# Attention numerators as products of 64 weight columns for each half of the partitions

## The chip, the cores and the metric

The kernel runs on one core of one Trainium2 chip. The metric is the device time of one execution in microseconds (us). Three runs of the kernel before took 924.83, 926.39 and 926.86 us; the median, 926.39 us, is the time before.

## The reference, cut to what matters

Three parts follow one another: a linear attention with random features, a feed-forward block with silu, and a gated feed-forward block. The change is in the attention. Its shapes are batch 4, 8 heads, 576 tokens, head dimension 64 and 128 features.

```python
q_p, k_p = (phi(q_s), phi(k_s))              # exp of a projection, less its row maximum
kv = np.einsum('bhsm,bhsd->bhmd', k_p, v)    # sums over the tokens of k and v
z = np.sum(k_p, axis=2)
num = np.einsum('bhsm,bhmd->bhsd', q_p, kv)  # the numerators
den = np.einsum('bhsm,bhm->bhs', q_p, z)[..., None] + 1e-06
return (num / den).astype(np.float32)
```

After it, `x = moe(x)` and `out = moe2(x)` are large matrix products (2304 tokens, width 512, inner widths 2048 and 1536).

## The kernel before, in words

**Tiling of the attention.** Two heads lie side by side on the 128 partitions (a pair), and two batches are taken together: a unit `u` is one pair of heads with two batches of 576 tokens, so 1152 tokens, which are nine chunks of 128. There are eight units, so 72 chunks, and the loop `step(s)` (L913) takes one chunk a step. As 576 is four and a half chunks, the fifth chunk of each unit holds the last 64 tokens of one batch and the first 64 of the next. The helper `runs` (L692) cuts a stretch of tokens at that border and gives, for each batch, its range `a` to `z` within the chunk.

**A step.** `proj(s + 1)` (L749) projects q and k of the next chunk: six products into a bank of PSUM, taken in turn out of five (`bank`, L669). `soft(s)` (L760) takes the four row maxima on DVE (L765) and four exponentials on ACT (L769), which read that bank. `kv_tr(s - 2)` (L779) adds the chunk's k to the sums of k and v (L789; 128 feature columns as weights, 65 columns of v with a column of ones as moving data) and turns q by two transposes (L805); ACT copies the turned q to SBUF (L816). On GpSimd (POOL), `split_piece` (L701) splits the loaded q and k into a high and a low part (L706, L708). Each engine works in the order in which the program gives it work. Between steps `feed` (L508) adds operations of the next stage: conversion of weights (POOL sums at L376, DVE operations at L350, L357, L406 and L419) and of the attention's output (POOL at L601, ACT at L571, DVE at L580). How many of them a step takes depends on the step's number, not on a clock.

**The numerators.** When the sums of a batch are complete, DVE copies them to SBUF (`kv_evac`, L821) as a 128 by 130 tile `st`: for each of the two heads 65 columns, of which one is the sum z. Then `tail` (L896) plans three groups of three chunks for each unit: `num(u, g)` (L835) makes the products, `divide` (L852) adds a small number to the sums, inverts and multiplies on DVE, two steps later `turn` (L864) transposes the result, and `take_out` (L870) copies it to SBUF. In `num`, the turned q of a chunk is the weight operand (128 features by up to 128 tokens) and `st` of that batch and head is the moving operand of 65 columns. The result stands at the tokens' partitions `a` to `z` of a PSUM bank, with 130 columns for each chunk. A chunk within one batch takes two products with 128 weight columns, one for each head. The fifth chunk takes four products with 64 weight columns: the two heads of the first batch on partitions 0 to 63, then the two heads of the second batch on partitions 64 to 127. The operands are fp32, and the hardware makes two weight loads and two products of each source product, so the trace has 320 records at L843 for 160 source products.

**The end of the attention.** For the last unit, `last_nums` (L994) makes two groups in one go when the next stage has begun, and two more products (`mark`, L1043) follow that wait for `divide`. The following stages are matrix products at L1066 and L1433, emitted in an order that a planner with fixed costs lays down before the run.

Of the kernel before, what the change touches and what calls it, by code (L numbers as in the profile page):

```python
# [42 lines left out]
def kernel(  # L43
# [13 lines left out]
    nc = tc.nc  # L57
    ctx.enter_context(tc.manual_schedule())
    P = 128
    DM, NT = outT.shape  # L60
    D, M = omT.shape
# [12 lines left out]
    VH = D + 1  # L74
# [607 lines left out]
    raw, hl, kq, qp, kvps = {}, {}, {}, {}, {}  # L682
# [9 lines left out]
    def runs(lo, hi):  # L692
        for b in range(lo // S, (hi - 1) // S + 1):
            a, z = max(lo, b * S), min(hi, (b + 1) * S)
            yield b, a - lo, z - lo, a == b * S, z == (b + 1) * S
# [123 lines left out]
    st = {}  # L819
# [15 lines left out]
    def num(u, g, to=None):  # L835

        pxs[u, g] = x = px.popleft() if to is None else to
        acc = ps[x]
        for c in range(g * GC, (g + 1) * GC):
            for b, a, z, _, _ in runs(c * P, (c + 1) * P):  # L840
                for h in range(2):
                    o = (c - g * GC) * VW + h * VH
                    nc.tensor.matmul(  # L843
                        acc[a:z, o : o + VH],
                        qp[u][:, h, c * P + a : c * P + z],
                        st[u, b][:, h * VH : (h + 1) * VH],
                        start=True,
                        stop=True,
                        skip_group_check=True,
                    )  # L850

    def divide(u, g):  # L852
        acc = ps[pxs[u, g]][:, : GC * VW].rearrange("p (c w) -> p c w", w=VW)
# [42 lines left out]
    def tail(u, b, s):  # L896
        if b and u == NU - 1:
            return
        for g, a in ((1, s + 2), (2, s + 6)) if b else ((0, s + 2 - (u == NU - 1)),):
            at(a, num, u, g)  # L900
            at(a, lambda g=g: dve_q.append(lambda: divide(u, g)))
            at(a + 2, turn, u, g)
            at(a + 2, lambda g=g: dve_q.append(lambda: take_out(u, g)))
            if g == GC - 1:
                at(a + 4, store, u)
# [88 lines left out]
    def last_nums():  # L994

        u = NU - 1
        num(u, 1, 7)
        num(u, 2, 6)
        divide(u, 1)
        divide(u, 2)  # L1000
        nc.scalar.activation(silu, silu, AF.Silu)
        clk["PE"] += 1.8
        clk["ACT"] = max(clk["ACT"], clk["PE"]) + 1.5
        clk["DVE"] = max(clk["DVE"], clk["PE"]) + 2.0
        actx.close()
        operands("rb")
        streams["x"].extend(to_come.pop(0)())
        later_on.append((5, lambda: last_turn(1)))
        later_on.append((7, lambda: last_turn(2)))
# [632 lines left out]
```

## Time and profile before

| what | value |
|---|---|
| median of three runs | 926.39 us |
| lowest and highest | 924.83 and 926.86 us |
| the profiled execution's own time | 926.11 us |
| its span, first to last instruction | 924.3 us |
| mean granted TensorE clock | 0.998 |
| DVE, ACT, POOL busy | 71%, 60%, 21% of the span |
| attention | from the start to about 150 us |

The engines are PE (TensorE's products), PEld (its weight loads, which overlap the products), DVE (VectorE), ACT (ScalarE), POOL (GpSimd) and SP (SyncE, which issues most DMAs). Ends of products are modelled, so for TensorE the starts are the safer reading: the distance from one start to the next is the time that the work took from the engine. A line such as L843 is a line of the kernel. A time in brackets behind a row is idle time of the engine ahead of that instruction, with what ended it.

### The profile page before, as it was taken

The page shows a single profiled execution, that of the slowest core. Times are in us where ns is not written, and L with a number is a line of the kernel's source. Part 1 is how long each engine was busy: PE and PEld are TensorE (multiplying, and loading weights), DVE is VectorE, ACT ScalarE, POOL GpSimd, SP SyncE. Part 2 cuts the span into 40 slices and gives each one's busy share as a digit, 9 for nine tenths or more (in the row PEclk, how much of TensorE's full clock was granted, in tenths as well). Part 3 has the DMA queues.
Part 4 walks back from the last instruction along what each step waited for, and adds up shares of the span by engine and source line. Part 5 has one row for each costly group of instructions (what it writes and reads, how often), then busy time and mean ns, then how long its engine had stood idle before and what let it go on. Part 6 is the DMA issues. An engine that isn't in the chain of part 4 may idle for free.

```text
span 924.3 us, 15768 instructions
## 1 busy us (share of the span) xinstructions
PE 905.0 (98%) x5591; PEld 895.3 (97%) x5591; DVE 657.7 (71%) x1055; ACT 558.4 (60%) x1190; POOL 197.0 (21%) x244
## 2 busy tenths in 40 slices
PE   8999999999999998999999999999999999999998
PEld 8999999999999998999999899999999999899998
DVE  4898986857574398586689899574747447968584
ACT  5788785876667675455457765554455447445453
POOL 6676951104343100000000014221303010000000
PEclk9999999999999999999999999999999999999999
DMA  7576515848989991715613755562626159371701
GB/s 218 183 235 208 174 50 197 271 157 275 317 291 358 349 382 58 232 55 163 206 43 109 244 164 187 174 201 79 213 68 222 47 184 314 114 240 52 237 16 69
DMA packets 109888, 169.94 MB, mean 184 GB/s; under 512 B 9200, under 2 KB 93808, under 8 KB 109808
## 3 DMA queue, kind: packets, MB, share of 16 engines
q1 hardware_dynamic: 108640, 168.33, 55.8%
q8 instruction: 44, 0.72, 0.3%
q10 hardware_dynamic: 1168, 0.59, 0.2%
q14 instruction: 36, 0.29, 0.1%
HBM read 107.02 MB, written 61.87 MB: 183 GB/s over the span
## 4 chain that ended last, share of the span: by engine, by line
PE 90%; DVE 4%; DMA 3%; ACT 2%; issue 1%; SPq 0%; DVEq 0%; ACTq 0%
PE ps L1066 43%; PE ps L1433 31%; PE ps L843 3%; PE ps L789 3%; PE ps L755 2%; PE ps L756 2%; PE ps L757 2%; PE ps L805 2%; DMA g_d<-fa 1%; PE ps L868 1%; DVE ra L1296 1%; DMA fa<-in_moe_w_in 1%; DVE ra L419 0%; DMA ra<-wu_val 0%; DVE fa L1124 0%
## 5 line engine op out<-in xcount | busy, mean ns | idle before, releaser
L376 POOL TENSOR_TENSOR fa<-fa 128x256 f32<-128x256 f32 x136 | 112.6, 841 | 529.0 <-DVE fa L357 301.3
L1066 PE MATMUL ps<-ra 128*128 128x384 f32 x840 | 156.3, 335 | 3.0 <-ACT ps L1083 3.0
L1066 PE MATMUL ps<-rb,ra 128*128 128x384 f32 x840 | 157.3, 340 | 0.0
L1066 PE MATMUL ps<-rc,ra 128*128 128x384 f32 x840 | 156.8, 339 | 0.0
L1066 PEld LDWEIGHTS ps<-ra 128*128 128x128 f32 x840 | 146.7, 188 | 4.3 <-ACT ps L1083 4.3
L1066 PEld LDWEIGHTS ps<-rb,ra 128*128 128x128 f32 x840 | 148.7, 188 | 0.3 <-ACT ps L1083 0.3
L1066 PEld LDWEIGHTS ps<-rc,ra 128*128 128x128 f32 x840 | 148.6, 188 | 0.1
L1083 ACT ACTIVATE ps<-ps 128x384 f32<-128x384 f32 x180 | 85.5, 476 | 88.7 <-PE ps L1066 82.1
L1140 DVE TENSOR_TENSOR fa<-fa,ps 128x384 f32<-128x384 f32 x120 | 66.2, 552 | 100.5 <-ACT ps L1083 78.1
L1292 ACT ACTIVATE ra<-fa 128x768 fp32r<-128x768 f32 x105 | 88.0, 844 | 81.2 <-PE ps L1433 64.4
L1296 DVE TENSOR_TENSOR ra<-fa,ra 128x768 fp32r<-128x768 f32 x105 | 100.5, 957 | 50.5 <-PE ps L1433 31.9
L1433 PE MATMUL ps<-ra,rb 128*128 128x384 f32 x720 | 129.4, 340 | 0.0
L1433 PEld LDWEIGHTS ps<-ra,rb 128*128 128x128 f32 x720 | 127.8, 189 | 0.8 <-DVE ra L1296 0.6
L1433 PE MATMUL ps<-ra 128*128 128x384 f32 x612 | 109.7, 337 | 6.7 <-DVE ra L1296 6.5
L1433 PEld LDWEIGHTS ps<-ra 128*128 128x128 f32 x612 | 106.7, 189 | 8.8 <-DVE ra L1296 8.0
L769 ACT ACTIVATE kq<-ps,nb 128x128 f32<-128x128 f32 x288 | 83.1, 403 | 25.3 <-DVE nb L765 24.1
L1433 PE MATMUL ps<-ra,rc 128*128 128x384 f32 x432 | 78.2, 340 | 1.6 <-DVE ra L1296 1.6
L1433 PEld LDWEIGHTS ps<-ra,rc 128*128 128x128 f32 x432 | 76.1, 188 | 2.7 <-DVE ra L1296 2.7
L1107 ACT ACTIVATE fa<-fa 128x384 f32<-128x384 f32 x84 | 43.8, 522 | 28.8 <-DVE fa L1140 28.5
L1316 DVE TENSOR_TENSOR fa<-ra,fa 128x768 f32<-128x768 f32 x63 | 60.1, 954 | 0.7
L1292 ACT ACTIVATE ra<-ra 128x768 fp32r<-128x768 f32 x42 | 35.5, 845 | 36.0 <-PE ps L1433 32.1
L1296 DVE TENSOR_TENSOR ra<-ra 128x768 fp32r<-128x768 f32 x42 | 40.2, 958 | 20.9 <-PE ps L1433 9.3
(100 smaller groups left out, 1227.6 us busy)
## 6 DMA issues: line engine op xcount, KB each, us to landing
g_d<-fa SPq DMA_DIRECT2D x168, 192.0 KB, 3.4
fa<-g_d SPq DMA_DIRECT2D x42, 384.0 KB, 4.4
ra<-g_d SPq DMA_DIRECT2D x42, 384.0 KB, 4.1
fa<-in_moe_w_out SPq DMA_DIRECT2D x28, 512.0 KB, 5.3
fa<-in_moe_w_in SPq DMA_DIRECT2D x16, 512.0 KB, 5.0
wd_out<-fa SPq DMA_DIRECT2D x14, 512.0 KB, 3.3
fa<-in_moe_w_gate SPq DMA_DIRECT2D x12, 512.0 KB, 3.9
fa<-in_moe_w_val SPq DMA_DIRECT2D x12, 512.0 KB, 5.2
```

The costliest lines, as they stand in the source:

```text
L376: f(blk(f"S{n}"), blk(l), blk(r))
L769: nc.scalar.activation(e[:, i, h * M : (h + 1) * M], ps[:, i, h * M : (h + 1) * M], AF.Exp, bias=nb[:, 2 * i + h : 2 * i + h + 1],)
L789: nc.tensor.matmul(acc[:, o : o + VH], e[a:z, 0, h * M : (h + 1) * M], v_t[u % 2][a:z, c, o : o + VH], start=first and h == 0, stop=last, ...
L843: nc.tensor.matmul(acc[a:z, o : o + VH], qp[u][:, h, c * P + a : c * P + z], st[u, b][:, h * VH : (h + 1) * VH], start=True, stop=True, sk ...
L1066: nc.tensor.matmul(ps[b][:, :N], cut(l, j * P, P), cut(r, j * N, N), start=start and c == 0, stop=stop and c == 5, skip_group_check=True,)
L1083: nc.scalar.activation(out() if callable(out) else out, src, AF.Copy)
L1107: nc.scalar.activation(b["t"], src, AF.Silu)
L1140: nc.vector.tensor_add(t, t if in_place else p5[n], ps[bank_][:, :N])
L1292: nc.scalar.activation(ops[s, p, k][0], src(), AF.Copy)
L1296: nc.vector.tensor_sub(l, src(), h.bitcast(F32))
L1316: (nc.gpsimd if eng == "POOL" else nc.vector).tensor_sub(z(PLACE[to]), z(PLACE.get(l, l)), z(PLACE.get(r, r)))
L1433: nc.tensor.matmul(ps[BANKS[p] + e][:, :N], cut(a, e * P, P), b, start=p in FIRST and i == 0 and c == 0, stop=p in LAST and i == fp - 1 an ...
```

## The change

In `num`, each product over the partitions `a` to `z` becomes one product for each 64 of them. A chunk within one batch now takes four source products with 64 weight columns: for the first head the partitions 0 to 63 and then 64 to 127, then the same for the second head. The fifth chunk of a unit is cut as before. The sums of k and v (L789) keep 128 weight columns.

```diff
                 for h in range(2):
                     o = (c - g * GC) * VW + h * VH
-                    nc.tensor.matmul(
-                        acc[a:z, o : o + VH],
-                        qp[u][:, h, c * P + a : c * P + z],
-                        st[u, b][:, h * VH : (h + 1) * VH],
-                        start=True,
-                        stop=True,
-                        skip_group_check=True,
-                    )
+                    for i in range(a, z, D):
+                        nc.tensor.matmul(
+                            acc[i : i + D, o : o + VH],
+                            qp[u][:, h, c * P + i : c * P + i + D],
+                            st[u, b][:, h * VH : (h + 1) * VH],
+                            start=True,
+                            stop=True,
+                            skip_group_check=True,
+                        )
```

Here `P` is 128, `D` 64, `VH` 65 and `VW` 130.

## Rows read from the trace of the kernel before

**Rows 1.** The page: busy time of the engines, and the chain's shares.
```profile
PE 905.0 (98%) x5591; PEld 895.3 (97%) x5591; DVE 657.7 (71%) x1055; ACT 558.4 (60%) x1190; POOL 197.0 (21%) x244
...
PE 90%; DVE 4%; DMA 3%; ACT 2%; issue 1%; SPq 0%; DVEq 0%; ACTq 0%
```

**Rows 2.** Groups by line and shape, PE, 0 to 260 us: busy, mean ns, idle.
```profile
L843 PE MATMUL ps<-st,qp 128*128 128x65 f32 x256 | 32.7, 272 | 0.0
...
L843 PE MATMUL ps<-st,qp 128*64 128x65 f32 x64 | 3.7, 234 | 0.0
```

**Rows 3.** Busy time by stretch: PE, PEld, DVE, ACT, POOL; clock, DMA share, GB/s.
```profile
75.00:80.00 5.00, 5.00 (x47) 5.00 (x47) 4.93 (x12) 4.24 (x15) 4.54 (x7) 1.00 0.28 64
...
85.00:90.00 5.00, 5.00 (x48) 4.80 (x47) 2.95 (x8) 5.00 (x18) 0.00 (x0) 1.00 1.03 359
...
95.00:100.00 5.00, 5.00 (x50) 4.86 (x50) 4.98 (x9) 3.78 (x14) 4.92 (x7) 1.00 0.55 170
100.00:105.00 5.00, 5.00 (x48) 4.80 (x47) 4.93 (x10) 3.86 (x12) 4.83 (x6) 1.00 0.64 184
```

**Rows 4.** Timeline of weight loads, a plain group: start, length, what, count.
```profile
70.75 1.42 PEld L843 LDWEIGHTS ps<-st,qp 128*128 128x128 f32 x12
72.09 0.19 PEld L755 LDWEIGHTS ps<-om_hi,hik 128*128 128x128 f32 x1
```

**Rows 5.** Timeline of weight loads: a mixed group, and two groups that adjoin.
```profile
63.34 1.50 PEld L843 LDWEIGHTS ps<-st,qp 128*128 128x128 f32 x16
64.76 0.19 PEld L755 LDWEIGHTS ps<-om_hi,hik 128*128 128x128 f32 x1
...
146.96 2.90 PEld L843 LDWEIGHTS ps<-st,qp 128*128 128x128 f32 x28
149.78 0.19 PEld L1043 LDWEIGHTS ps<-ra 128*128 128x128 f32 x1
```

**Rows 6.** Timeline of the mixed group, narrow windows; each row begins where its window does.
```profile
63.34 0.27 PE L805 MATMUL ps<-ident,kq 128*128 128x128 f32 x1
...
63.73 0.28 PE L843 MATMUL ps<-st,qp 128*128 128x65 f32 x1
...
63.93 0.32 PEld L843 LDWEIGHTS ps<-st,qp 128*64 128x64 f32 x8
...
63.94 0.25 PEld L843 LDWEIGHTS ps<-st,qp 128*64 128x64 f32 x5
...
64.11 0.14 PEld L843 LDWEIGHTS ps<-st,qp 128*64 128x64 f32 x1
...
64.32 0.19 PEld L843 LDWEIGHTS ps<-st,qp 128*128 128x128 f32 x1
```

**Rows 7.** Busy time of L843 alone by stretch: PE, PEld with counts.
```profile
20.00:98.00 78.00, 19.20 (x172) 18.24 (x172) 1.00 0.63 200
98.00:107.30 9.30, 3.01 (x28) 2.78 (x28) 1.00 0.66 195
107.30:152.00 44.70, 13.09 (x120) 12.52 (x120) 1.00 0.34 107
```

**Rows 8.** Waits from 20 to 150 us: total us, times, longest.
```profile
ACT kq L769 <- DVE nb L765: 16.1, 23, 1.4
DVE rc L855 <- PE ps L843: 12.3, 15, 2.5
```

**Rows 9.** Timelines of POOL and of DVE: start, length, what, idle time before.
```profile
65.48 0.51 POOL L706 TENSOR_SCALAR hik<-rawk 128x384 fp32r<-128x384 f32 x1 [1.97 <-PE ps L757]
...
75.22 0.73 POOL L376 TENSOR_TENSOR fa<-fa 128x256 f32<-128x256 f32 x1 [2.52 <-DVE fa L357]
...
90.04 0.73 POOL L376 TENSOR_TENSOR fa<-fa 128x256 f32<-128x256 f32 x1 [5.18 <-DMA rawk<-in_k]
...
97.00 1.18 POOL L376 TENSOR_TENSOR fa<-fa 128x256 f32<-128x256 f32 x1
...
98.21 1.21 DVE L406 CAST ra<-fa 128x512 fp32r<-128x512 f32 x1
```

## The prediction, made before the changed kernel ran

> **What bounds the kernel now.** I read the page's engine lines and its chain first: TensorE is busy in 98% of the span and carries 90% of the chain [rows 1]. A busy TensorE alone would prove little, so the grouping by line and shape comes next: the numerator products of L843 are 256 records with 128 weight columns and 64 with 64 columns, and TensorE never stood idle ahead of either [rows 2]. Every source product leaves two records there, so this is 128 plain products and the 32 that the program already makes on half the partitions. The stretches of 5 us show PE at 5.00 of 5.00 throughout the attention, while DVE is at 4.93 to 4.98 in several of them and POOL at 4.92 in one [rows 3]. So in this stage TensorE sets the pace, and two engines stand just behind it. That gives two questions: what do the products of L843 cost TensorE, and how much of a gain do DVE and POOL let through?
>
> **What a group costs today.** TensorE's queue is read by the starts of its weight loads, since products overlap and their ends are modelled. A plain group (three chunks, twelve records) runs from the first load at 70.75 to the next line's first load at 72.09: 1.34 us, 0.112 for each load with its product [rows 4]. The group with the chunk that crosses two batches holds eight records of 128 columns and eight of 64, and takes 64.76 − 63.34 = 1.42 [rows 5].
>
> **What halves cost.** That crossing chunk is the change in small. Its eight records of 64 columns: the first load starts at 63.93, the second at 63.94, the eighth at 64.11 [rows 6]. Loads start in pairs 0.01 apart: two streams, one for each half of the array, run side by side, and in each of them three steps take 64.11 − 63.94 = 0.17, so 0.057 a step. In program order the second half's products stand four behind, so TensorE reached ahead for them. Getting in and out costs extra. The last product of 128 columns starts at 63.73 and the first half load at 63.93, 0.20 later. The last half load of the first stream starts near 64.10 and the next load of 128 columns at 64.32, 0.22 later [rows 6]. In the changed kernel the line ahead is the transpose of L805, whose last product starts at 63.34, just where L843's first load starts today [rows 5, 6].
>
> So a group after the change has 24 records, twelve in each stream, and takes 0.20 + 11 × 0.057 + 0.22 = **1.05 us**. Against 1.34 a plain group saves 0.29, against 1.42 a mixed one 0.37. There are 24 groups, 16 plain and 8 mixed: 4.6 + 3.0 = 7.6. At two places (u = 6 and the last) two groups adjoin, one of them the row of 28 records with 149.78 − 146.96 = 2.82 [rows 5]. There one exit and one entry fall away, 0.20 + 0.22 − 0.057 = 0.36 each, 0.7 together. **Gross gain: 8.3 us.** Nothing else moves: no DMA, wait or operation of another engine is added, and the 128 extra source products (256 loads and products) are the ones just counted. Before the numerators nothing is queued that the change delays; behind them come the next projections and, on DVE, the division, which waited 12.3 us for L843 and gets its input earlier [rows 8].
>
> **What is given back.** By place, 172 records of L843 start before 98 us, 28 from there to 107.3 and 120 behind that [rows 7]. In groups: nine plain and four mixed before (2.6 + 1.5 = 4.1 us of gain), one of each between (0.7), the rest behind (3.6, with both adjoining places).
>
> Ahead of 98 PE's lead runs into the other engines. POOL waited for PE last at length at 65.48 (1.97 us). At 75.22 it waited 2.52 for DVE, and from 90.04, where a DMA released it, it works without a break: the sum of L376 that begins at 97.00 ends at 98.18, and DVE's L406 starts at 98.21 [rows 9]. L406 is in DVE's queue ahead of softmax maxima and divisions, ACT's exponentials follow those maxima (16.1 us of waits) [rows 8], and PE's next projection needs the bank that the exponentials free. So at 98 the lead of PE can't exceed POOL's lead by more than the little slack in between. POOL's lead is at most PE's at 65, eight groups or 5 × 0.29 + 3 × 0.37 = 2.6, less what DVE, with 0.07 spare in 75 to 80, couldn't follow [rows 3]. The trace shows no way to read PE's slack directly, so I bound it. Everything kept gives 8.3. If nothing won before 107 survives, only the 3.6 behind it remain. I take a lead of 1.9 at 98 (nearer to 2.6 than to nothing, because POOL and DVE do have gaps before 65), nothing from the two groups between, where DVE has 0.02 and 0.07 of 5 us spare [rows 3], and all of the 3.6 behind, where it has room: 1.9 + 3.6 = **5.5 us**. After the attention PE stays the bound and the lead is carried to the end.
>
> The profiled execution took 926.11 us (span 924.3). Less 5.5 that is 920.6; the median of the three runs is 0.28 above it, so I forecast **920.9 us**.
>
> **Rivals.**
> 1. *All is kept.* For it: PE shows no idle time at all. Against: rows 9 tie DVE to POOL at 98. It would give 926.39 − 8.3 = 918.1. Chance 0.13.
> 2. *DVE and POOL take back everything won before 107.* Only 3.6 remains: 922.8. For it: DVE's 4.93 and 4.98 [rows 3]. Against: DVE is at 2.95 in 85 to 90 [rows 3], and POOL's wait for PE at 65.48 shows that it can move up. Chance 0.09.
> 3. *The halves take turns (slower).* Halves overlap in today's chunk because four products of one half stand in a row; here they alternate after every source product, and a group is longer than what is queued ahead. If TensorE then runs one record at a time at 0.057, a plain group takes 0.20 + 23 × 0.057 + 0.22 = 1.73, 0.39 more than now. Over the 24 groups, with 0.31 for a mixed one and 0.36 less at each of the two adjoining places, that is 6.2 + 2.5 − 0.7 = 8.0 us: 934.4. It decides from a mean start to start of (1.34 − 0.42) / 23 = 0.040 us over both halves; rows 6 show 0.18 / 7 = 0.026. Against it: those rows, where the half further back in the program was reached within 0.01. Chance 0.06. The Trainium skill (TensorE: Matmul & The Clock Gate, section "Wait — 56ns, not 53.3ns?") says that with hardware decode off the sequencer spends about 62 ns on a product and binds once the array's work is shorter; by that a group would take 24 × 62 = 1.49 us, an estimate, longer than today. The eight records of rows 6, at 0.026, speak against it; no row shows a run of 24.
> 4. *Nothing to measure*, since entry and exit cost nearly what halves save, or the pace lies between. Within 0.2% of 926.4 (1.9 us, about what a measurement of this kernel tells from no change). Chance 0.06.
>
> **How the numbers follow.** The forecast's case (a gain between 4 and 7, 919.4 to 922.4) has 0.66, rival 1 0.13, rival 2 0.09, rival 3 0.06, rival 4 0.06. Faster by more than 0.2% are the first three: 0.88; same 0.06; slower 0.06. The range takes in the forecast's case and rivals 1 and 2 with half a microsecond around their values: 917.6 to 923.3.
>
> **What would show it.** Right: L843 has only 64-column records, 512 of them; a plain group's loads take about 1.05 from first to next line, in pairs of starts 0.01 apart. PE waits appear around 98 to 107, 1 to 2 us in all, for ACT's exponentials or DVE; a DVE at its limit stands behind them. The marks of L1043 come near 144.3 instead of 149.78, and everything after stands earlier by that same amount. A POOL that runs on end from about 88 shows the limit I named. Wrong on the pace: single starts 0.05 or more apart, or a group over 1.2 us. Wrong on the give-back: no PE waits and L1043 at 141.5, or PE waits spread over the whole attention. A lead that shrinks after 150 would mean that a stage I took for PE-bound isn't.

## The result, and the profile of the changed kernel

The changed kernel takes 917.96 us (median of 6 runs, 917.2 to 919.7) against 926.36 us (6 runs, 924.83 to 928.57) for the kernel before in the same comparison: a ratio of 0.9911 [0.9895, 0.9927], so by the ratio 8.2 us faster with an interval of 6.8 to 9.7 (by the medians 8.4). Forecast were 920.9 us, in a range from 917.6 to 923.3. The profiled execution took 918.76 us, 0.8 more than the median, with a span of 917.0, 7.3 less than the span before, at a granted clock of 0.998 in both. The readings below account for those 7.3 us.

The page of the changed kernel, which answers to [rows 1]:

```profile
PE 897.4 (98%) x5847; PEld 883.6 (96%) x5847; DVE 654.4 (71%) x1055; ACT 558.5 (61%) x1190; POOL 198.5 (22%) x244
...
PE 85%; DVE 7%; DMA 3%; ACT 3%; issue 1%; POOL 0%; SPq 0%; DVEq 0%; ACTq 0%
```

TensorE has 256 more records, is still busy in 98% of the span, and has handed 5% of the chain to other engines, 3% of it to DVE. The grouping by line and shape, 0 to 260 us, shows the numerators, which are L844 here, with one shape only; this answers to [rows 2]:

```profile
L844 PE MATMUL ps<-st,qp 128*64 128x65 f32 x576 | 22.0, 226 | 0.0
```

Busy time doesn't show the gain, since two streams overlap. The starts of the weight loads do. The timeline of the weight loads (start, length, what, count, idle time before it): a plain group, a mixed one, one stall, and the two groups that adjoin at the end. It answers to [rows 4, 5].

```profile
68.69 0.78 PEld L844 LDWEIGHTS ps<-st,qp 128*64 128x64 f32 x24 [0.17 <-issue]
69.54 0.19 PEld L755 LDWEIGHTS ps<-om_hi,hik 128*128 128x128 f32 x1
...
78.09 0.83 PEld L844 LDWEIGHTS ps<-st,qp 128*64 128x64 f32 x24 [0.17 <-DVE ra L580]
78.99 0.19 PEld L755 LDWEIGHTS ps<-om_hi,hik 128*128 128x128 f32 x1
...
100.94 0.19 PEld L755 LDWEIGHTS ps<-om_hi,hik 128*128 128x128 f32 x1 [0.77 <-ACT kq L769]
...
141.09 1.53 PEld L844 LDWEIGHTS ps<-st,qp 128*64 128x64 f32 x48 [0.25 <-issue]
142.69 0.19 PEld L1044 LDWEIGHTS ps<-ra 128*128 128x128 f32 x1
```

A plain group takes 0.85 from its first half load to the next line, a mixed one 0.90, the row of 48 records 1.60. The 0.17 of idle time is the entry: from the start of the last transpose's product to the first half load it is 0.20. The releaser that one of these rows names (DVE L580) is a chance neighbour, because the same 0.17 stands before groups with "issue". The row at 100.94 is the only other stall of TensorE between 20 and 134 us. The mark that followed the attention's last products stood at 149.78 [rows 5]; it stands at 142.69 now, 7.1 earlier.

With one stall the account closes. I took the distance from one step's first load of L755 to the next step's, for the 63 steps in which this can be read, in both kernels and in the experiment e4 below:

| step | before | after | e4 |
|---|---|---|---|
| with a plain group | 2.67 | 2.38 | 2.38 |
| with a mixed group | 2.76 | 2.43 | 2.43 |
| the step that ends at 100.94 | 1.68 | 2.48 | 1.68 |
| sum saved in the 63 steps | | 5.43 | 6.23 |

The other steps agree within 0.03 us. The first of the adjoining pairs then saves 0.93 (2.68 before, 1.55 and an entry of 0.20 after), the last 0.95. Gross that is 6.23 + 0.93 + 0.95 = 8.1 us; less the 0.80 of the stall, 7.3. The attention began 0.23 later in this execution, which is why the mark stands only 7.1 earlier; the other 0.2 of the span came behind the mark and isn't traced to a cause.

Where the 0.80 comes from is on the other engines' timelines (POOL, then DVE, then ACT; rows of the changed kernel that answer to [rows 9] and follow on them):

```profile
63.22 0.51 POOL L706 TENSOR_SCALAR hik<-rawk 128x384 fp32r<-128x384 f32 x1 [1.86 <-PE ps L757]
...
72.89 0.73 POOL L376 TENSOR_TENSOR fa<-fa 128x256 f32<-128x256 f32 x1 [2.51 <-DVE fa L357]
...
86.77 0.72 POOL L376 TENSOR_TENSOR fa<-fa 128x256 f32<-128x256 f32 x1 [4.32 <-DVE rc L856]
...
93.75 1.17 POOL L376 TENSOR_TENSOR fa<-fa 128x256 f32<-128x256 f32 x1
...
94.95 1.21 DVE L406 CAST ra<-fa 128x512 fp32r<-128x512 f32 x1
...
97.56 0.71 DVE L419 TENSOR_TENSOR ra<-fa,ra 128x512 fp32r<-128x512 f32 x1
98.19 0.85 DVE L580 TENSOR_TENSOR ra<-fa,ra 128x384 fp32r<-128x384 f32 x1
98.97 0.68 DVE L765 TENSOR_REDUCE nb<-ps 128x4 f32<-128x512 f32 x1
...
99.75 1.14 ACT L769 ACTIVATE kq<-ps,nb 128x128 f32<-128x128 f32 x4 [0.77 <-DVE nb L765]
```

Read it by differences to [rows 9]. POOL's lead over its old times is 2.26 at 63.22, 2.33 at 72.89, 3.27 at 86.77 and 3.25 at 93.75: behind 86.77 it works without a break and the lead stays. What made it grow between 72.89 and 86.77 is a transfer. The sum at 86.77 writes a buffer of which there is only one, and it has to wait until the buffer's old contents have been stored by a DMA, `wd_out<-fa` of L435 (the releaser that the row names, DVE L856, ended by chance at the same moment, and the transfer that the row of [rows 9] names was likewise only a neighbour). Its issue and its time to landing, before the change and after it:

```profile
83.25 0.75 SPq L435 DMA_DIRECT2D wd_out<-fa  x1
wd_out<-fa SPq DMA_DIRECT2D x1, 512.0 KB, 6.7
...
80.86 0.62 SPq L435 DMA_DIRECT2D wd_out<-fa  x1
wd_out<-fa SPq DMA_DIRECT2D x1, 512.0 KB, 5.8
```

The store was issued 2.39 earlier than before the change, and it landed 3.27 earlier (by the trace's records at 86.64 instead of 89.91), as it took 5.78 us instead of 6.66, which the view rounds. In both kernels POOL's sum starts 0.13 after the landing. So 2.4 of POOL's lead came with the earlier issue and 0.9 with the shorter transfer.

DVE's L406 starts 0.03 after the end of the sum at 93.75, as it did before, 98.21 − 94.95 = 3.26 earlier. From there DVE works on end through the two fed operations L419 and L580 to the maxima at 98.97; ACT's exponentials follow them and end at 100.89, and TensorE's projection starts at 100.94. TensorE's own saving had grown to 4.33 by then. It began its attention 0.23 later in this execution (first L755 of the account at 19.10, not 18.87), so it stood 4.1 ahead by the clock, ran into an engine that stood 3.3 ahead, and paid 0.80. The windows show the same stretches as [rows 3], with the same columns:

```profile
75.00:80.00 5.00, 5.00 (x62) 4.76 (x60) 4.63 (x9) 5.00 (x18) 4.75 (x7) 1.00 0.74 223
...
85.00:90.00 5.00, 5.00 (x77) 4.53 (x76) 4.31 (x12) 4.53 (x15) 3.14 (x4) 1.00 0.54 183
...
95.00:100.00 5.00, 5.00 (x60) 4.73 (x57) 4.93 (x9) 4.23 (x13) 4.92 (x6) 1.00 0.85 266
100.00:105.00 5.00, 4.47 (x56) 3.82 (x56) 4.93 (x11) 4.44 (x17) 4.75 (x6) 1.00 0.46 120
```

PE leaves 5.00 in one of them, where DVE is at 4.93 and POOL at 4.75. The waits between 20 and 150 us answer to [rows 8]:

```profile
ACT kq L769 <- DVE nb L765: 11.8, 19, 1.6
...
DVE rc L856 <- PE ps L844: 7.0, 10, 2.0
```

The division waits 5.3 us less for the numerators: the engines behind TensorE followed it by giving up idle time, until one of them had none left to give.

### The profile page after: what moved, and what is told of

Read it like the earlier page. It is cut to its first block, busy times and chain, and to the rows that moved or that the text cites. A ratio compares the mean times of both kernels' runs of the same rounds, so it can differ in the third digit from the quotient of the medians.

```text
span 917.0 us, 16280 instructions
## 1 busy us (share of the span) xinstructions
PE 897.4 (98%) x5847; PEld 883.6 (96%) x5847; DVE 654.4 (71%) x1055; ACT 558.5 (61%) x1190; POOL 198.5 (22%) x244
## 4 chain that ended last, share of the span: by engine, by line
PE 85%; DVE 7%; DMA 3%; ACT 3%; issue 1%; POOL 0%; SPq 0%; DVEq 0%; ACTq 0%
PE ps L1067 44%; PE ps L1434 31%; PE ps L789 2%; PE ps L755 2%; PE ps L844 1%; PE ps L756 1%; PE ps L757 1%; PE ps L805 1%; DMA g_d<-fa 1%; DVE nb L765 1%; DVE ra L1297 1%; DVE ra L419 1%; ACT kq L769 1%; PE ps L869 1%; DMA fa<-in_moe_w_in 1%
```

## The experiments

The theory after the result: the halves run as two streams, one step of 0.057 us for each record of a half, with 0.20 and 0.22 for entry and exit; and the work that `feed` puts on POOL and DVE takes back 0.8. The main rivals: the streams share a limit (the sequencer or the loads), or the loss is a cost of TensorE's own. As the attention's start differs between executions (by up to 1.7 us here), I compare the stretch from the first numerator's start to that of the first adjoining pair: 21.63 to 140.55, so 118.92 us before, and 21.95 to 135.44, 113.49 us after the change.

**e1_first_half_twice**: each product for partitions 0 to 63 is made twice. Extra work of one half only.

```diff
                     for i in range(a, z, D):
+                        for _ in range(2 if i == 0 else 1):
```

> Every product on partitions 0 to 63 is made twice in a row, those on 64 to 127 once; the result is the same. Theory (two streams side by side, each at 0.057 us a step, so a group lasts as long as the longer stream): a group has 24 steps in one stream and 12 in the other and takes 0.20 + 23 x 0.057 + 0.22 = 1.73 us instead of 1.05; the 24 groups add 24 x 0.68 = 16 us, of which DVE's and POOL's limit hides at most one: 932 to 934 us. Rival (the records run one after another at about 0.026, only cheaper than 128 columns): 0.42 + 35 x 0.026 = 1.33 us a group, 925 us.

A plain group's weight loads in e1 (timeline, columns as above):

```profile
74.90 1.47 PEld L845 LDWEIGHTS ps<-st,qp 128*64 128x64 f32 x36 [0.17 <-issue]
76.44 0.19 PEld L755 LDWEIGHTS ps<-om_hi,hik 128*128 128x128 f32 x1
```

From load to next line 1.54, with the entry 1.74, and 934.51 us in one run (half a microsecond above the range that theory gave) beside 927.6 for the kernel before. Twelve more records of one half lengthen the group by 0.69, 0.057 each. So one half's records follow one another at that step, and the longer stream sets the group.

**e2_both_halves_twice**: both halves' products are made twice.

```diff
                     for i in range(a, z, D):
+                        for _ in range(2):
```

> Every product of both halves is made twice in a row; the result is the same. Theory (two streams): 24 steps in each stream, the same 1.73 us a group as with one half doubled, so the same time as that run within 1 us, 932 to 934 us: the second half's twelve more steps cost nothing. Rival (one after another at 0.026): 0.42 + 47 x 0.026 = 1.64 us a group, some 7 us more than with one half doubled.

The same view of e2:

```profile
75.36 1.53 PEld L845 LDWEIGHTS ps<-st,qp 128*64 128x64 f32 x48 [0.17 <-issue]
76.96 0.19 PEld L755 LDWEIGHTS ps<-om_hi,hik 128*128 128x128 f32 x1
```

Twelve more records than in e1, all of the other half, cost 1.60 − 1.54 = 0.06. They run beside the first half's: no shared limit shows at 0.033 us a record. The whole took 936.5, 2.0 more than e1, above the at most 1 us that theory gave. The plain groups make 16 × 0.06 = 1.0, as theory had it. It missed the mixed groups, which take 1.83 from load to next line against 1.54 in e1, 2.3 over the eight of them (by groups that is more than 3, where the two single executions differ by 2.0). In their crossing chunk eight records of one half stand in a row, and the streams get out of step. That order matters is what e3 tests.

**e3_half_after_half**: the same products, but all of a group's first half before all of its second.

```diff
+        for i in (0, D):
-        for c in range(g * GC, (g + 1) * GC):
-            for b, a, z, _, _ in runs(c * P, (c + 1) * P):
+            for c in range(g * GC, (g + 1) * GC):
+                for b, a, z, _, _ in runs(c * P, (c + 1) * P):
...
-                    for i in range(a, z, D):
+                        if a <= i < z:
```

> The same products in another order: all twelve records of a group on partitions 0 to 63, then all twelve on 64 to 127. Theory (TensorE reaches ahead to the other half over the whole group): 1.05 us a group, 918 us as with the change. Rival A (it reaches ahead over about eight records, as in the chunk that crosses batches of the kernel before, where the first record of the second half stood four places behind): the second stream starts about four to eight steps late, a group takes 1.3 to 1.5 us, 923 to 928 us. Rival B (it doesn't reach ahead that far at all, the halves follow one another): 1.73 us a group, 934 us.

Weight loads of e3, a plain group, whole and by 72.9 us, and the starts of its products by 73.222 and by 73.23:

```profile
72.70 1.30 PEld L845 LDWEIGHTS ps<-st,qp 128*64 128x64 f32 x24 [0.17 <-issue]
74.07 0.19 PEld L755 LDWEIGHTS ps<-om_hi,hik 128*128 128x128 f32 x1
...
72.70 0.31 PEld L845 LDWEIGHTS ps<-st,qp 128*64 128x64 f32 x4 [0.17 <-issue]
...
72.70 0.74 PE L845 MATMUL ps<-st,qp 128*64 128x65 f32 x9
...
72.70 0.79 PE L845 MATMUL ps<-st,qp 128*64 128x65 f32 x10
```

Four loads had begun by 72.9, 0.2 us into the group: one stream alone. The records don't name their half, but their steps tell the halves apart: nine products start 0.06 or more apart, and the tenth starts 6 ns after the ninth. It is the second half's first, and it has passed the last three of the first half's twelve. In the crossing chunk of [rows 6] the second half's first record also passed three that had to wait. So between the halves TensorE doesn't keep to the order of the program, but its reach ahead is short. The group takes 1.37 + 0.20 = 1.57, longer than the 1.34 of the kernel before and a little above the range of rival A, which it is nearest to; its step is 2.89, where the account above has 2.67 and 2.38. The last numerator of the attention starts at 153.6, where it was 149.7 before the change. The whole took 928.06 beside 927.6; the span is 2.0 longer than that of the profile before, so about half of the 3.9 us was made up behind the attention, and this case doesn't show where. The rival named "halves take turns" doesn't hold for the change as it stands, but the gain hangs on the order: the same products in another order lose it all.

**e4_nothing_fed**: the two `feed` calls of the steps are left out, so the fed work comes after the attention's steps; its whole time (961.49) therefore isn't comparable and only the stretch is read.

```diff
-            if s >= 8:
-                feed("conv", s, {"SP": 1, "ACT": 1, "DVE": 1, "POOL": 1})
-            if s >= 27:
-                feed("x", s, {"SP": 4, "ACT": 2, "DVE": 2, "POOL": 1})
```

> With the change; the steps of the attention get no operations of the next stage (conversion of weights, splitting of the attention's output); these follow after the attention, so the whole time is much longer and isn't compared. What is read is where the last pair of groups inside the attention begins (48 records): at 140.4 before the change (weight loads) and at 135.4 with it, a lead of 5.1 us where the groups ahead of it gained 6.2 to 6.4 by themselves. Theory (the missing 1.2 us were taken by DVE and POOL with the fed work): with nothing fed it begins at 134.0 to 134.3, and TensorE waits for nothing between 20 and 134. Rival (the loss lies in the attention's own chain of maxima and exponentials, or the gain of a group is smaller): it begins at 135 or later, with the wait near 100 still there.

TensorE's waits from 20 to 140 us in e4 (us in all, times, longest):

```profile
PEld ps L844 <- issue: 3.5, 21, 0.2
```

Only the entries of the 21 rows of half products are left: the wait near 100 us is gone, though nothing in the products changed. The stretch is 135.23 − 22.54 = 112.69, 0.80 less than with the change, and every step of the account above agrees with the changed kernel's except the one with the stall. The absolute start of the last pair, 135.23, missed theory's 134.0 to 134.3 and by the letter matches the rival's "135 or later". For 0.6 of that the attention itself began later; the other 0.3 are an overestimate of the loss, 1.2 us where the steps show 0.80. So the fed work took back 0.8, and nothing else was lost.

**e5_quarters**: products of 32 weight columns, four streams.

```diff
-                    for i in range(a, z, D):
+                    for i in range(a, z, D // 2):
...
-                            acc[i : i + D, o : o + VH],
-                            qp[u][:, h, c * P + i : c * P + i + D],
+                            acc[i : i + D // 2, o : o + VH],
+                            qp[u][:, h, c * P + i : c * P + i + D // 2],
```

> Four products of 32 weight columns in place of two of 64, in the order of the four quarters for each head; the result is the same. Theory from the order experiment (a stream is set by its weight columns, but TensorE reaches only about four records ahead, and each source product brings two for the same quarter): at most three of four quarters run at once, 48 records at 0.02 to 0.03 us each on average, a group of 0.42 + 47 x 0.02 to 0.03 = 1.4 to 1.8 us if a step keeps some 0.057, or near 1.0 if a step shrinks to 0.03: so 917 to 935 us, no gain. Rival (four streams at full overlap and half the step): 0.42 + 11 x 0.03 = 0.75 us a group, 7 us less than with 64 columns before DVE's and POOL's share, 912 us.

Weight loads of a plain group in e5, and the products that have started by 36.06:

```profile
36.02 0.73 PEld L844 LDWEIGHTS ps<-st,qp 128*32 128x32 f32 x48 [0.17 <-issue]
36.84 0.19 PEld L755 LDWEIGHTS ps<-om_hi,hik 128*128 128x128 f32 x1
...
36.02 0.26 PE L844 MATMUL ps<-st,qp 128*32 128x65 f32 x4
```

0.82 instead of 0.85, for twice as many records: 918.57 us (4 runs), ratio 0.9916 [0.9897, 0.9935], no better than the change. Each quarter must still make its twelve records of 65 moving columns, and a stream's step is 0.057 again (the group's 48 products start in twelve bursts of four). What the change won is that a stream of 64 columns takes 0.057 a record where 128 columns took 0.112; a further halving doesn't repeat that. So the time met theory's range, but not by its reasoning, which had at most three quarters run at once. Here 48 records begin within 0.82 us, 0.017 each, and the 24 records of the plain group of the change within 0.78 us, 0.03 each. The Trainium skill (TensorE: Matmul & The Clock Gate, section "Wait — 56ns, not 53.3ns?") says that with hardware decode off the sequencer spends about 62 ns on a product. Neither run shows that limit; whether hardware decode was off here, no run shows.

**e6_sums_in_halves_too**: in the steps with numerators, the transposes of q come first, then the sums of k and v (L789) as two halves of 64 weight columns, then the numerators, so that the array enters and leaves the halves once.

```diff
+        if nums and whole:
+            turn_q()
...
-                nc.tensor.matmul(
-                    acc[:, o : o + VH],
-                    e[a:z, 0, h * M : (h + 1) * M],
+                w = D if nums and whole else P
+                for i in range(0, P, w):
+                    nc.tensor.matmul(
+                        acc[i : i + w, o : o + VH],
+                        e[a:z, 0, h * M + i : h * M + i + w],
```

> With the change, and in the 21 steps in which numerators follow, the transposes of q go first and the sums of k and v are made as products of 64 weight columns for each half, right ahead of the numerators, so that the way into the halves is paid once. The result is the same. Theory (a step of each stream 0.057 us, no second way in or out): four records of 128 columns at 0.112 become four steps at 0.057, 0.22 us less in each of 21 steps, 4.6 us on TensorE, of which about 1 is taken by DVE and POOL near 100 us: 914 to 915 us. Rival (a sum must now wait for q's exponentials behind the transposes, or the sums' halves don't run side by side): 918 us or more, with waits of TensorE at the transposes or the sums.

TensorE's waits from 20 to 150 us in e6 (rows of the view of all waits):

```profile
PEld ps L755 <- ACT kq L769: 2.0, 4, 1.2
...
PEld ps L755 <- POOL fa L601: 0.7, 1, 0.7
...
PEld ps L881 <- DVE nt L871: 0.6, 2, 0.5
```

917.53 us (6 runs), ratio 0.9914 [0.9896, 0.9931]; the stretch is 134.64 − 21.07 = 113.57, as with the change. The sums' products became shorter (the numerators follow 0.28 after the sums begin, with no second entry), and TensorE's waits on ACT, POOL and DVE grew from 0.8 to 3.3, most of what e8 below finds the half sums to be worth. These waits are at the projections and at `turn` (L881), not at the transposes or the sums, so the rival's reason doesn't hold either; theory had the cause of the loss, but far too little of it.

**e7_crossing_chunk_alternates**: in the chunk that crosses two batches, the head becomes the outer loop, so the halves alternate there too.

```diff
-            for b, a, z, _, _ in runs(c * P, (c + 1) * P):
-                for h in range(2):
-                    o = (c - g * GC) * VW + h * VH
+            for h in range(2):
+                o = (c - g * GC) * VW + h * VH
+                for b, a, z, _, _ in runs(c * P, (c + 1) * P):
```

> With the change; in the chunk that crosses two batches the halves alternate too (the head is the outer loop, the batch the inner one). The result is the same. Theory (TensorE reaches about four records ahead, so four in a row for one half cost the other one step): the mixed groups take as long as the plain ones, 0.85 us from their first load to the next line's instead of 0.90, 8 x 0.05 = 0.4 us less in all: within what the timing can tell. Rival (the 0.05 has another cause, as the second batch's tile): the mixed groups stay at 0.90.

Weight loads of a mixed group in e7:

```profile
28.29 0.78 PEld L844 LDWEIGHTS ps<-st,qp 128*64 128x64 f32 x24 [0.17 <-issue]
29.14 0.19 PEld L755 LDWEIGHTS ps<-om_hi,hik 128*128 128x128 f32 x1
```

0.85, as a plain group, where the change takes 0.90: the 0.05 of each mixed group is the order of its four products. The whole is 917.88 us (5 runs), ratio 0.9917 [0.9899, 0.9935]. The 0.4 us don't show: the stall near 101 grew from 0.8 to 1.3. In this execution the store of L435 took 6.3 us, and the sum of POOL that waits for it came 0.45 later than with the change:

```profile
87.22 0.94 POOL L376 TENSOR_TENSOR fa<-fa 128x256 f32<-128x256 f32 x1 [5.25 <-DMA rawk<-in_k]
```

So the larger stall can't be put down to the 0.05 a group alone.

**e8_sums_in_halves_nothing_fed**: e6 and e7 without the `feed` calls; as in e4 the fed work comes after the attention's steps, and only the stretch is read.

> The sums in halves and the alternating crossing chunk, with no operations of the next stage fed to the steps of the attention (they follow after it, so the whole time isn't compared). What is read is the time from the first product of the first group to the first of the last pair of groups inside the attention: 118.9 us before the change, 113.5 with it, 112.7 with it and nothing fed, 113.6 with the sums in halves. Theory (the gain of the sums in halves was taken by DVE and POOL with the fed work): 19 or 20 x 0.22 = 4.3 us less than 112.7, and 0.3 for the crossing chunks: 108.1 us, no waits of TensorE. Rival (the attention's own maxima, exponentials and splits are the limit, or the sums' halves gain nothing): 111 us or more, with waits.

TensorE's waits from 20 to 130 us in e8:

```profile
PEld ps L807 <- issue: 3.3, 20, 0.2
```

The stretch is 130.91 − 21.82 = 109.08. Against e4 that is 3.6 us less, 0.35 of it from seven mixed groups at 0.05. Half sums alone are worth over 3 us of TensorE's time here; with the fed work (e6) none of it is left. The value lies nearer to theory's 108.1 than to the rival's 111, and the rival's waits are absent.

**e10_change_x_later and e11_before_x_later**: the fed conversion of the attention's output begins with step 48 instead of 27, in the changed kernel (e10) and in the kernel before (e11). e11 is the control: if TensorE alone set the pace before, the same relief is worth nothing there.

```diff
-            if s >= 27:
+            if s >= 48:
                 feed("x", s, {"SP": 4, "ACT": 2, "DVE": 2, "POOL": 1})
```

> The change alone, with the attention's output split from step 48 on instead of 27. Theory: the wait of TensorE near 101 us (0.8 us) goes and the pair of groups at the end comes 0.8 us earlier, 112.7 us behind the first group: 917.2 us. Rival (the wait moves): 113.5 us behind the first group, 918 us.

> The kernel before, with the attention's output split from step 48 on instead of 27: the control. Theory (before the change TensorE alone sets the pace): 118.9 us from the first group to the last pair, 926 us, the same as before. Rival (fed work already cost TensorE time before): earlier by 0.5 us or more.

The window of e10 that answers to 100 to 105 us above, and POOL's sum behind the store of L435:

```profile
100.00:105.00 5.00, 5.00 (x76) 4.53 (x76) 3.82 (x11) 5.00 (x18) 3.73 (x5) 1.00 0.94 285
...
84.49 0.73 POOL L376 TENSOR_TENSOR fa<-fa 128x256 f32<-128x256 f32 x1 [3.41 <-DMA wd_out<-fa]
```

PE is back at 5.00 and DVE at 3.82; the stall near 101 is gone (a wait of 0.2 stands at 116), and the stretch is 134.44 − 21.41 = 113.03, between theory's 112.7 and the rival's 113.5. The later conversion does two things at once, which this run can't part: POOL and DVE have less to do near 100 us, and the store of L435 is issued 2.0 earlier and lands in 5.5 us, so that POOL's sum starts at 84.49 instead of 86.77. The whole is 916.77 us (4 runs), ratio 0.9912 [0.9899, 0.9926]; the half microsecond is too little for the whole time to show. e11: 926.18 us (11 runs), ratio 1.0003 [0.9993, 1.0013], stretch 141.23 − 22.08 = 119.15. So before the change the moved work cost nothing, and the trace of the kernel before lists no wait of TensorE's weight loads from 20 to 150 us.

**e9_sums_in_halves_x_later**: the half sums of e6, the order of e7 and the later conversion of e10 together.

> The sums in halves and the alternating crossing chunk; the attention's output is split for the next stage from step 48 on instead of step 27, when the conversion of weights is nearly done, so that DVE and POOL have less to do near 95 to 105 us and more after. The result is the same. Theory (DVE and POOL near 100 us took the gain): some 2 to 3 us of the 4.6 come back, 914 to 916 us, and the wait of 1.2 us near 101 goes. Rival (POOL's and DVE's work is only moved to where it stops TensorE later): 917 to 919 us.

Waits of TensorE from 20 to 134 us in e9:

```profile
PEld ps L755 <- ACT kq L769: 1.4, 4, 0.4
PEld ps L755 <- POOL fa L376: 0.9, 1, 0.9
```

916.07 us (4 runs, 915.48 to 916.48), ratio 0.9899 [0.9884, 0.9914]: the lowest median of all, though its interval overlaps the change's, and just above theory's 914 to 916. The wait near 101 shrank to 0.4, but others came, one of 0.9 on POOL among them. The stretch is 134.81 − 22.16 = 112.65, 3.6 more than in e8, so the fed work that remains still takes most of what half sums give.

## Why the prediction was right, and where it was not

- **The range.** 917.96 lies inside it, but only 0.4 above its lower end, which the range owes to the first rival. The forecast's own case, a gain of 5.5 us, fell short of the measured 8.2.
- **TensorE sets the pace, and every group's saving counts.** Right: the account closes at 8.1 gross, against 8.3 forecast. The kernel before had no wait of TensorE's weight loads from 20 to 150 us, and relief of the other engines was worth nothing there (e11).
- **A plain group at 1.05 us.** Right to the hundredth: 0.85 and the entry of 0.20. e1 and e2 confirm its terms one by one: 0.057 for a record of the longer stream, nearly nothing for the other.
- **A mixed group at 1.05 us.** 1.10 by its loads. I counted twelve records in each stream but took no notice of their order; four of one half in a row cost 0.05 (e7). Over 8 groups that is 0.4, and half of it shows in the gross gain, 8.1 against 8.3; the plain groups saved a little more than 0.29 and the steps without numerators 0.1 in all. The signs of being right also named 512 records of 64 columns; there are 576, because the 64 of the crossing chunks are among them. The sum used the right number, 24 a group.
- **The give-back near 98 to 107.** The mechanism was named rightly: POOL that works on end, DVE tied to it, then maxima, exponentials, and a wait of TensorE's projection. The size was not: 2.8 us forecast, 0.8 measured. The step that failed is the lead at 98 us: "POOL's lead is at most PE's at 65", 2.6, of which 1.9 was taken. POOL's lead at 93.75 is 3.25. Up to the store that POOL waits for, the bound held: POOL stands 2.26 and 2.33 ahead, the issue of the store 2.39, so POOL had followed TensorE more closely than the 1.9 supposed. The prediction saw that a DMA releases POOL at 90.04, but gave that transfer no term. It took 0.88 less than before, and POOL's lead grew by that much. This part is luck: the same store took 5.5 to 7.1 us in the executions with fed work, and why is not shown. With the 6.66 of the kernel before, POOL's lead would have stayed near 2.4 and the stall would have been about 1.7 instead of 0.8 (an estimate, 4.10 − 2.39). The other executions point the same way without proving it: a landing in 6.3 us stands beside a stall of 1.3 (e7), one in 7.1 beside stalls of 0.6 and 1.2 (e5), an earlier landing beside none (e10). No run changes the transfer alone.
- **Nothing from the two groups between.** The mixed one is part of TensorE's lead of 4.33 ahead of the stall. The plain one comes behind the stall and kept its whole 0.31. So of what was won before 107 us 4.33 − 0.80 + 0.31 = 3.8 survived, forecast 1.9.
- **Behind 107 all is kept.** Right: 1.59 in the steps, 0.93 and 0.95 at the two pairs, 3.5 in all, forecast 3.6. The lead at the mark is 7.1 and at the end 7.3. That a lead at the mark always arrives in full isn't shown: of e3's delay only half did.
- **The signs.** Of PE waits 1 to 2 us were foreseen, 0.8 came. The mark was to stand near 144.3, or at 141.5 if nothing is given back; at 142.69 it is nearer to the second.
- **Rivals.** "All is kept" gave 918.1, and the median is 917.96; the number fits better than mine, though its reason doesn't hold: the profile has a stall of 0.8 that e4 and e10 take away. By profiled executions the gain is 7.3, between that rival's 8.3 and my 5.5. "Everything won before 107 is taken back" is refuted by 7.1 at the mark. "The halves take turns" is refuted for this order, and e3 shows under which order it comes near.

## What to carry to other kernels

Where a row of products has 128 weight columns and few moving ones (shown here for fp32 products with 65), try halving the weights so that the halves write different partitions, and let them alternate after every product; price it as two streams, with entry and exit paid once per row, so put such rows next to one another. When an engine gets faster, find for each follower its last idle time before it works without a break: there its lead is set, by whatever ends that idle time. If that is a DMA, the lead is only as sure as the transfer's time, and the give-back wants a range for it. Then relieve the followers before making the same engine faster again: half sums were worth over 3 us to TensorE and nothing that could be measured to the kernel while the fed work stayed in place (e6), and with part of that work moved most of it stayed out of reach (e9).

## What the runs showed of the hardware beyond what was expected

- To start the other half's products TensorE passed three records that had to wait, and in e3, where eleven stood ahead of the second half's first when the group began, it took that one only when three were left; [rows 6] shows the same distance. In e5 the first four products, one of each quarter, start within 0.02 us, which again passes three. Where the other half was within reach, both started 0.01 us or less apart.
- Quarters ran as four streams, but took 0.82 where halves took 0.85 (e5). Between 128 and 64 weight columns the step of a stream fell from 0.112 to 0.057 us; with 32 it was 0.057 again. Why it doesn't fall further was not tested.
- One and the same store of 512 KB (L435) took 5.5 to 7.1 us from issue to landing in the executions with fed work, 6.66 in the profile before and 5.78 in that of the change; its landing set the time of everything POOL did next.
